# One table for ScalarE's softmax steps in a fused dynamic-convolution and maxout kernel

## The chip, the core and the metric

The kernel runs on one core of a Trainium2 chip. The core has five engines with a queue each: TensorE (PE, matrix products; PEld is its loading of weights), VectorE (DVE), ScalarE (ACT), GpSimd (POOL) and SyncE (SP). They run side by side and wait for one another through semaphores. An engine takes its instructions in the order in which the program issued them. [...]

The metric is the time of one execution on the device in microseconds (us), lower is better. The kernel before takes 410.58 us, the median of three runs (410.37 to 411.28).

## The reference

For each of 8 x 4160 positions a softmax over 7 taps is taken for each of 8 heads, and the 192 channels (24 to a head) are filtered with these taps, over the position itself and the six before it. Then a maxout layer follows:

```python
w = np.exp(weight_gen - max); w = w / (sum(w) + 1e-09)      # 8 heads x 7 taps a position
out = np.einsum('bshk,bskhg->bshg', w, x_unf)               # a causal convolution, 192 channels
h1 = x @ w1                                                  # 192 -> 1024
h2 = x @ w2
g = np.maximum(h1, h2)
return (g @ w_out).astype(np.float32)                        # 1024 -> 192
```

There are 33,280 positions in all. Types outside are float32; the kernel works in bfloat16 where it multiplies.

## The kernel before

The 33,280 positions stand on 128 partitions, 260 columns each. The columns are cut into 17 batches: 16 of 16 columns, and a last one of 4 (`BATCHES`). From the third batch on a batch goes through the engines in two halves (units) of 8 columns; a half begins at column 0 or 8 of its batch.

**The softmax steps of a batch c.** ScalarE takes the exponential of the raw weights (`exp_sum`, L135; named X.c here), VectorE adds up the seven taps of each head (`red`, L147, in two parts), ScalarE takes the logarithm of the sums (`ln`, L151; l.c), VectorE subtracts it from the raw weights (`shift`, L156, in three parts), and ScalarE takes the exponential again (`weights`, L167; W.c.0 for the first half, W.c.8 for the second). So X.c goes to both parts of red, these to l.c, that to shift, and shift to W.c.0 and W.c.8.

**The convolution of a half.** VectorE multiplies inputs by weights (`mul`, L182) and adds the taps in three steps (`adds`, L198, L202, L205). The parts of red for a batch further on stand between these steps of a second half, and the parts of shift between those of a first half. The last addition gives y_t. SyncE's queue issues a DMA that transposes it to yt (`transpose`, L214), with channels on the partitions.

**The maxout on TensorE.** The sum is split as max(h1, h2) = h1 + relu(h2 - h1). The linear part has its own matrix w10 (L347). A tile is one of 8 equal pieces of a half's hidden layer: `hid_tile` (L295) multiplies by the difference of the two weight matrices into one of three PSUM tiles, hda, hdb and hdc, and ScalarE's relu (L305) moves it to SBUF as rd_t. Output columns are added up in PSUM as op_ps (L347, then L335 in two parts, `out_first` and `out_second`), and ScalarE copies them to o_t (`evac`, L391). There is one tile op_ps from group 8 on, so TensorE's first product of a group's output waits for the copy of the group before.

**Groups.** TensorE's work runs in groups (`GROUPS`): 8 of two tiles, then 82 of three or fewer, so that batch 2 begins in group 13. Each group makes its tiles and adds up the output of earlier ones, two or four columns (`OUTS`), from group 23 on by turns. In `hidden` the order on TensorE is hda, hdb, first part of the output, hdc, second part. ScalarE's order is relu of hda, relu of hdb, an empty instruction (`relay`) that tells TensorE that the first part is through, relu of hdc, and the copy.

**Where the softmax steps go.** Up to batch 2, and for l.3, X.3, they are written out by hand. From W.3 on, the code before gives each step a due tile: a formula with the batch number, `AT` with six exceptions, and in `softmax_steps` a rule that puts a long step (X or W) off by a group when the group has four columns and the last one had a long step, but for the groups that start at the tiles in `NOW`. The function `steps` runs them through `beside`, ahead of VectorE's work in `extra`. In a group of four columns `beside` stands before the relu of hdc; in a group of two, behind the copy:

```python
        if len(now) > 2:
            beside()
        relu(rd, t0 + n - 1, 1)
...
            evac(now[0] // 2, len(now) // 2)
        between()
        if len(now) <= 2:
            beside()
```

Of the kernel before, what the change touches and what calls it, by code (L numbers as in the profile page):

```python
# [17 lines left out]
def _sub(base: bass.AP, off: int, dims):  # L18
    ap = [list(base.ap[0])] + [[int(s), int(c)] for s, c in dims]
    return dataclasses.replace(base, offset=base.offset + off, ap=ap)  # L20
# [3 lines left out]
def kernel(  # L24
# [26 lines left out]
    NB = len(BATCHES)  # L51


    def pieces(b):
        n = BATCHES[b][1]
        at, done = [], 0
        for w in (4, 4, 4, 4) if b < 2 else (8, 8) if n == 16 else (n,):
            at.append((done, w))
            done += w
        return at  # L60
# [10 lines left out]
    GROUPS = [(t, 2) for t in range(0, 16, 2)]  # L71
# [59 lines left out]
    def exp_sum(b, i=0, of=1):  # L131
        if i == 0:
            e_ts[b] = pe_.tile([P, BATCHES[b][1] * WGC], FP32, name="e_t", tag="e")
        w = BATCHES[b][1] * WGC // of
        nc.scalar.activation(out=e_ts[b][:, i * w:(i + 1) * w], in_=wg_ts[b][:, i * w:(i + 1) * w], func=AF.Exp)  # L135

    def part(b, i, of):

        n = BATCHES[b][1]
        h0, h1 = n * i // of * H, n * (i + 1) // of * H  # L140
        return slice(h0, h1), h0 * K, [[K, h1 - h0], [1, K]]
# [7 lines left out]
    def ln(b, i=0, of=1):  # L149
        s_t = s_ts[b][:, part(b, i, of)[0]]  # L150
        nc.scalar.activation(out=s_t, in_=s_t, func=AF.Ln)  # L151
# [7 lines left out]
    def weights(b, o):  # L159

        w = dict(pieces(b))[o]
        if b not in en_ts:
            en_ts[b] = pen.tile([P, 16 * WGC * 2], BF16, name="en_t", tag="en")
        J = 2 if w == 4 and b < 2 else 1
        N = w * H // J
        for j in range(J):
            nc.scalar.activation(  # L167
                out=_sub(en_ts[b], (o * WGC + j * N * K) * 2, [[2 * N, K], [2, N], [1, 2]]),
                in_=_sub(wg_ts[b], (o * H + j * N) * K, [[1, K], [K, N], [0, 2]]), func=AF.Exp,
            )  # L170
# [60 lines left out]
    def half(j):  # L231
        return slice(64 * j, 64 * j + 64)
# [33 lines left out]
    def chunks(t):  # L266

        u, k = TILES[t]
        return ([k], 512) if UNITS[u][2] == 8 else ([2 * k, 2 * k + 1], 256)

    def hid_out(t, f, j):

        fs, w = chunks(t)
        hd, at = hd_at[t]
        at += j * 512 + fs.index(f) * w
        return hd[:, at:at + w]
# [5 lines left out]
    def wd_at(j, s, h, c0, n):  # L282

        at = WD[h, j, s] * HF + c0
        return wd[half(j), at:at + n]

    def hid_tile(t):


        u = TILES[t][0]  # L290
        fs, w = chunks(t)
        for f in fs:
            for s in range(3):
                for j in range(2):
                    nc.tensor.matmul(  # L295
                        hid_out(t, f, j), lhsT=wd_at(j, s, f // 4, f % 4 * P, P),
                        rhs=_sub(yt_ts[u][half(j), :], (s + j) % 3 * P, [[3 * P, w // P], [1, P]]),
                        start=(f == fs[0] and s == 0), stop=(f == fs[-1] and s == 2),
                        skip_group_check=True,
                    )  # L300
# [40 lines left out]
    def out_first(now):  # L341

        for c in now[::2]:
            u, i, _ = column(c)
            for s in range(3):
                for j in range(2):
                    nc.tensor.matmul(  # L347
                        op_out(c + j),
                        lhsT=yt_ts[u][half(j), (3 * i + (s + j) % 3) * P:(3 * i + (s + j) % 3 + 1) * P],
                        rhs=w10[half(j), s * D:(s + 1) * D], start=(c == now[0] and s == 0),  # L350
                        stop=False, skip_group_check=True,
                    )
            for f in range(FCH):
                last = [out_hidden(c + j, f, j) for j in range(2)]
        return last
# [10 lines left out]
    def relay(last):  # L366

        go = nc.scalar.nop()
        for mm in last:
            tc.add_manual_dep(go.ins, mm.ins.name, SYNC, reason="bank of the other half")  # L370
        return go
# [52 lines left out]
    OUTS, c = [[], [], []], 0  # L424
    for g in range(3, len(GROUPS)):
        most = 4 if g == 3 else 2 if GROUPS[g][1] == 2 or len(OUTS[-1]) == 4 else 4
        n = min(most, ready[g] - c)
# [5 lines left out]
    def room(g):  # L433

        t0, n = GROUPS[g]
        if "c" in ps:
            for t, k in zip(range(t0, t0 + n), "abc"[:n - 1] + "c"):
                hd_at[t] = ps[k].tile([P, 1024], FP32, name="hd" + k, tag=k), 0
        else:
            for t in range(t0, t0 + n):  # L440
                hd_at[t] = ps["h"].tile([P, 1024], FP32, name="hdp", tag="hd"), 0
        rd = prd.tile([P, 3 * 1024], BF16, name="rd_t", tag="rd")
        for t in range(t0, t0 + n):
            rd_at[t] = (rd, t - t0)
        return rd

    def out_room(now, tag=None):
        tag = tag or ("r" if "r" in ps else "o")
        tile_ = ps[tag].tile([P, 1024], FP32, name="op_ps", tag=tag if tag in "abc" else "op")
        for c in now:  # L450
            op_at[c // 2] = tile_, (c - now[0]) // 2 * D

    def hidden(g, now=(), between=lambda: None, beside=lambda: None, ahead=lambda: None):


        t0, n = GROUPS[g]
        rd = room(g)
        for t in range(t0, t0 + n - 1):
            hid_tile(t)
        if now:  # L460
            out_room(now, "a" if n == 1 and "a" in ps else None)
            last = out_first(now)
        for t in range(t0, t0 + n - 1):
            relu(rd, t, 1)
        if now:
            go = relay(last)
        hid_tile(t0 + n - 1)
        if len(now) > 2:
            beside()
        relu(rd, t0 + n - 1, 1)  # L470
        ahead()
        if now:
            out_second(now, go)
            evac(now[0] // 2, len(now) // 2)
        between()
        if len(now) <= 2:
            beside()

# [214 lines left out]
    def end_of_1():  # L693
# [13 lines left out]
        7: (lambda: (sum_transpose(7)), none),  # L707
    }

    NOW = (28, 40, 49)  # L710
    AT = {
        ('W', 8, 8): 115,
        ('W', 11, 8): 163,
        ('W', 14, 8): 211,
        ('X', 6, 0): 49,
        ('X', 5, 0): 37,
        ('W', 3, 8): 30,
    }
    due = {}
    for c in range(3, NB):  # L720
        soon = c < 8
        parts_ = [(AT.get(('W', c, 0), 16 * (c - 2) + (8 if soon else 10 if c < NB - 1 else 15)), True, lambda c=c: weights(c, 0))]
        if 8 in dict(pieces(c)):
            parts_.append((AT.get(('W', c, 8), 16 * (c - 2) + (14 if soon else 15)), True, lambda c=c: weights(c, 8)))
        if c > 3:
            ln_at = -2 if c == 4 else 0 if c < 8 else 2 if c < 11 else 4
            parts_.append((AT.get(('l', c, 0), 16 * (c - 2) + ln_at), False, lambda c=c: ln(c)))
            parts_.append((AT.get(('X', c, 0), 16 * (c - 3) + (4 if c < 8 else 7)), True, lambda c=c: exp_sum(c)))
        for t, *step in parts_:
            due.setdefault(t, []).append(step)  # L730
    waiting, long_in_two = [], [False]

    def softmax_steps(g):

        t0, n = GROUPS[g]
        for t in range(max(t0, 16), t0 + n):
            waiting.extend(due.get(t, ()))
        two = len(OUTS[g]) <= 2
        put_off = [w for w in waiting if w[0] and not two and long_in_two[0] and t0 not in NOW]
        now = [w for w in waiting if w not in put_off]  # L740
        waiting[:] = put_off
        for _, step in now:
            step()
        long_in_two[0] = two and any(long for long, _ in now)

    def extra(t):

# [17 lines left out]

    def steps(g, tiles):

        if tiles:
            softmax_steps(g)
        for t in tiles:  # L770
            extra(t)

# [5 lines left out]
    for g in range(4, len(GROUPS)):  # L778
        if GROUPS[g][1] == 3 and "c" not in ps:
            later_ps()  # L780
        tiles = [t for t in range(GROUPS[g][0], sum(GROUPS[g])) if t >= 16]
        if g == 9:
            behind(relu_of[16], load_x(3, 0, 8))
        if g in early:
            hidden(g, OUTS[g], early[g][0], ahead=lambda: {4: lambda: (weights(1, 12), ln(2)), }.get(g, none)())
            early[g][1]()
            steps(g, tiles)
        else:
            hidden(g, OUTS[g], beside=lambda: steps(g, tiles))
    rest_of_results(OUTS[-1])  # L790

# [28 lines left out]
```

## Time and profile before

| | before |
|---|---|
| median of three runs | 410.58 us (410.37 to 411.28) |
| the profiled execution | 409.7 us |
| its span on the core | 407.9 us |
| VectorE busy | 370.6 us (91%) |
| ScalarE busy | 361.4 us (89%) |
| GpSimd busy | 74.9 us (18%) |
| TensorE's granted clock | 1.00 |

The span runs from the program's first instruction to its last; 1.8 us of the execution lie around it. The profile's page lists each engine's busy time, the chain of work that ended last, the groups of instructions and their idle time. The trace behind it has every instruction: a row of the timeline gives its start and its length in us, the engine, the line of the kernel, the operation, the tile that is written, the tile that is read, and how often; in brackets behind it, how long the engine had been idle and what ended that. TensorE's matmuls overlap, so a block of them is best read by the time from its start to the next block's start.

### The profile page before, as it was taken

What the parts mean: (1) busy time and instruction counts of PE and PEld (TensorE: products, weight loads), DVE (VectorE), ACT (ScalarE), POOL (GpSimd) and SP (SyncE); (2) the same over time, 40 slices, a digit from 0 to 9 for tenths busy, and PEclk for the clock granted to TensorE, in tenths of its full rate; (3) what the DMA queues carried; (4) which work ended last, traced back from release to release, by engine and by line L of the source; (5) the groups of instructions that cost most, each with busy time, mean ns of one, the idle gap of its engine ahead of it and who ended that gap; (6) DMA issues with size and microseconds to landing.
All of it is one profiled execution on the core that took longest, in us unless ns stands there. A gap on an engine that the chain in (4) does not pass through costs nothing.

```text
span 407.9 us, 16236 instructions
## 1 busy us (share of the span) xinstructions
PE 398.3 (98%) x7458; PEld 317.9 (78%) x7458; DVE 370.6 (91%) x215; ACT 361.4 (89%) x462; POOL 74.9 (18%) x101
## 2 busy tenths in 40 slices
PE   7999999999999999999999999999999999999996
PEld 2689999777777877777787778877787777777795
DVE  5999997999999999999999999999999999999100
ACT  5899889999999999989999999999999889887872
POOL 0311012222211022212102222221122212010000
PEclk9999999999999999999999999999999999999999
DMA  8957497667647854964785497478649647853614
GB/s 240 233 127 212 120 151 162 161 149 183 150 98 213 211 133 101 257 152 104 206 229 123 93 262 172 81 235 215 106 98 258 167 53 248 149 98 85 209 38 159
DMA packets 60785, 65.70 MB, mean 161 GB/s; under 512 B 47631, under 2 KB 49039, under 8 KB 60718
## 3 DMA queue, kind: packets, MB, share of 16 engines
q1 hardware_dynamic: 52334, 40.54, 35.4%
q0 software_dynamic: 8240, 24.04, 29.6%
q8 instruction: 58, 0.95, 0.9%
q10 hardware_dynamic: 144, 0.10, 0.1%
q14 instruction: 9, 0.07, 0.1%
HBM read 35.96 MB, written 25.56 MB: 151 GB/s over the span
## 4 chain that ended last, share of the span: by engine, by line
DVE 66%; PE 23%; issue 5%; ACT 4%; DMA 1%; DVEq 0%; SPq 0%
DVE m_t L182 32%; DVE m_t L198 15%; DVE m_t L202 10%; PE op_ps L335 9%; DVE y_t L205 3%; DVE sum_t L147 3%; PE warm L605 3%; DVE wg_t L156 3%; PE hdc L295 2%; PE hda L295 2%; ACT rd_t L305 2%; PE hdb L295 2%; PE op_ps L347 2%; PE yps L244 2%; PE hdp L295 1%
## 5 line engine op out<-in xcount | busy, mean ns | idle before, releaser
L335 PE MATMUL op_ps<-wo,rd_t 64*128 64x192 bf16 x4160 | 210.7, 243 | 0.5 <-issue 0.4
L335 PEld LDWEIGHTS <-rd_t 64*128 64x128 bf16 x4160 | 180.5, 94 | 16.7 <-issue 0.6
L182 DVE TENSOR_TENSOR m_t<-xb_t,en_t 128x10752 bf16<-128x10752 bf16 (+1 forms) x37 | 187.5, 5071 | 3.1 <-ACT en_t L167 2.8
L295 PEld LDWEIGHTS <-wd 64*128 64x128 bf16 x1776 | 92.9, 94 | 41.9 <-issue 2.1
L305 ACT ACTIVATE rd_t<-hdc 128x1024 bf16<-128x1024 f32 x82 | 84.0, 1025 | 20.4 <-PE hdc L295 18.5
L222 POOL CAST gate<-yt 128x1 f32<-128x1 bf16 x29 | 40.3, 1389 | 263.7 <-DMA yt<-y_t 263.7
L305 ACT ACTIVATE rd_t<-hda 128x1024 bf16<-128x1024 f32 x81 | 83.4, 1030 | 0.4 <-PE hda L295 0.4
L305 ACT ACTIVATE rd_t<-hdb 128x1024 bf16<-128x1024 f32 x81 | 83.6, 1032 | 0.0
L198 DVE TENSOR_TENSOR m_t<-m_t 128x4608 bf16<-128x4608 bf16 (+1 forms) x29 | 72.7, 2508 | 0.1
L295 PE MATMUL hdc<-yt,wd 64*128 64x512 bf16 (+1 forms) x534 | 67.9, 359 | 0.7 <-DMA yt<-y_t 0.7
L391 ACT COPY o_t<-op_ps 128x384 f32<-128x384 f32 (+1 forms) x99 | 55.9, 576 | 13.9 <-PE op_ps L335 13.9
L295 PE MATMUL hda<-yt,wd 64*128 64x512 bf16 (+1 forms) x528 | 67.1, 359 | 0.2 <-DMA yt<-y_t 0.2
L295 PE MATMUL hdb<-yt,wd 64*128 64x512 bf16 (+1 forms) x522 | 67.1, 361 | 0.0
L347 PE MATMUL op_ps<-w,yt 64*128 64x192 bf16 x780 | 55.4, 243 | 0.4 <-ACT w L658 0.4
L347 PEld LDWEIGHTS <-yt 64*128 64x128 bf16 x780 | 38.7, 94 | 16.1 <-issue 0.8
L202 DVE TENSOR_TENSOR m_t<-m_t 128x3072 bf16<-128x3072 bf16 (+1 forms) x29 | 49.9, 1722 | 0.1
L167 ACT ACTIVATE en_t<-wg_t 128x896 bf16<-128x896 f32 (+2 forms) x45 | 35.1, 806 | 0.6 <-PE op_ps L335 0.6
L205 DVE TENSOR_TENSOR y_t<-m_t 128x1536 bf16<-128x1536 bf16 (+1 forms) x29 | 27.3, 940 | 0.5
L114 POOL DMA_DIRECT2D xb_t<-in_x_dram x33 | 17.7, 535 | 31.5 <-ACT rd_t L305 20.4
L156 DVE TENSOR_TENSOR wg_t<-wg_t,sum_t 128x280 f32<-128x280 f32 (+5 forms) x46 | 22.0, 481 | 0.3 <-ACT sum_t L151 0.3
L147 DVE TENSOR_REDUCE sum_t<-e_t 128x64 f32<-128x448 f32 (+2 forms) x31 | 19.6, 633 | 2.9 <-ACT e_t L135 2.8
L135 ACT ACTIVATE e_t<-wg_t 128x896 f32<-128x896 f32 (+2 forms) x18 | 15.9, 887 | 2.7 <-DMA wg_t<-in_weight_gen_dram 2.7
(49 smaller groups left out, 118.3 us busy)
## 6 DMA issues: line engine op xcount, KB each, us to landing
out_dram<-o_t SPq DMA_DIRECT2D x27, 768.0 KB, 5.2
xb_t<-in_x_dram POOLq DMA_DIRECT2D x30, 384.0 KB, 4.9
wg_t<-in_weight_gen_dram POOLq DMA_DIRECT2D x14, 448.0 KB, 5.3
xb_t<-xb_t POOLq DMA_DIRECT2D x16, 288.0 KB, 5.1
out_dram<-o_t SPq DMA_DIRECT2D x10, 384.0 KB, 2.9
wg_t<-in_weight_gen_dram SPq DMA_DIRECT2D x2, 448.0 KB, 4.6
xs<-in_x_dram SPq DMA_DIRECT2D x2, 384.0 KB, 5.9
xb_t<-in_x_dram POOLq DMA_DIRECT2D x3, 192.0 KB, 4.2
```

The source lines that it names most:

```text
L156: nc.vector.tensor_tensor(out=w_t, in0=w_t, in1=_sub(s_ts[b], hs.start, [[1, hs.stop - hs.start], [0, K]]), op=ALU.subtract)
L167: nc.scalar.activation(out=_sub(en_ts[b], (o * WGC + j * N * K) * 2, [[2 * N, K], [2, N], [1, 2]]), in_=_sub(wg_ts[b], (o * H + j * N) * K ...
L182: return nc.vector.tensor_tensor(out=m_out, in0=x_in, in1=_sub(en_ts[b], o * WGC * 2, [[2, K * n * H], [0, G // 2], [1, 2]]), op=ALU.mult,)
L198: nc.vector.tensor_tensor(out=taps(0, 1, 3), in0=taps(0, 1, 3), in1=taps(3, 1, 3), op=ALU.add)
L202: nc.vector.tensor_tensor(out=taps(0, 2, 2), in0=taps(0, 2, 2), in1=taps(1, 5, 2), op=ALU.add)
L205: nc.vector.tensor_tensor(out=_sub(y_ts[b], o * D, [[64, 2], [P, 3 * w // 2], [1, 64]]), in0=taps(0, 1, 1), in1=taps(2, 1, 1), op=ALU.add,)
L222: nc.gpsimd.tensor_copy(out=gate, in_=yt[:, 0:1])
L295: nc.tensor.matmul(hid_out(t, f, j), lhsT=wd_at(j, s, f // 4, f % 4 * P, P), rhs=_sub(yt_ts[u][half(j), :], (s + j) % 3 * P, [[3 * P, w // ...
L305: relu_of[t0] = nc.scalar.activation(out=rd[:, k * 1024:(k + n) * 1024], in_=hd[:, at:at + n * 1024], func=AF.Relu)
L335: return nc.tensor.matmul(op_out(c), lhsT=rd[half(r), k * 1024 + at:k * 1024 + at + P], rhs=wo[half(r), f * D:(f + 1) * D], start=False, s ...
L347: nc.tensor.matmul(op_out(c + j), lhsT=yt_ts[u][half(j), (3 * i + (s + j) % 3) * P:(3 * i + (s + j) % 3 + 1) * P], rhs=w10[half(j), s * D: ...
L391: nc.scalar.copy(out=_sub(o, c % 24 * D, [[D, len(qs)], [h * D, 2], [1, D]]), in_=_sub(tile_, at + (qs[0] - p) * D, [[D, len(qs)], [512, 2 ...
```

## The change

All softmax steps from W.3 on come from one table, `SOFTMAX_AT`, by group and place. Place 0 is before the relu of a group's last tile, place 1 behind the copy, and now each of them can be had in any group. VectorE's `extra` stays where it was.

```diff
@@ hidden
+               before=lambda: None, after=lambda: None):
...
         hid_tile(t0 + n - 1)
+        before()
         if len(now) > 2:
             beside()
         relu(rd, t0 + n - 1, 1)
...
         between()
+        after()
         if len(now) <= 2:
             beside()
@@
-    def softmax_steps(g):
...
-        put_off = [w for w in waiting if w[0] and not two and long_in_two[0] and t0 not in NOW]
...
+    SOFTMAX_AT = {
+        (9, 1): "X.4 W.3.0", (12, 0): "W.3.8 l.4", (15, 1): "X.5", (16, 0): "W.4.0", (16, 1): "l.5",
+        (18, 1): "W.4.8", (19, 0): "X.6", (21, 1): "W.5.0", (23, 1): "W.5.8 l.6", (25, 1): "X.7",
+        (27, 1): "W.6.0", (29, 0): "l.7", (29, 1): "W.6.8 X.8", (33, 1): "W.7.0", (34, 0): "l.8",
+        (35, 1): "W.7.8", (37, 1): "X.9 W.8.0", (39, 1): "W.8.8", (40, 0): "l.9", (41, 1): "X.10",
+        (43, 1): "W.9.0", (44, 1): "l.10", (45, 1): "W.9.8", (47, 1): "X.11", (49, 1): "W.10.0",
+        (51, 0): "l.11", (51, 1): "W.10.8 X.12", (53, 1): "W.11.0", (55, 1): "W.11.8", (56, 0): "l.12",
+        (57, 1): "X.13", (59, 1): "W.12.0", (61, 1): "W.12.8", (62, 0): "l.13", (63, 1): "X.14",
+        (65, 1): "W.13.0", (67, 1): "W.13.8 l.14", (69, 1): "X.15 W.14.0", (72, 0): "l.15",
+        (73, 1): "W.14.8 X.16", (76, 0): "W.15.0", (78, 0): "l.16", (79, 1): "W.15.8", (82, 0): "W.16.0",
+    }
+
+    def softmax_steps(g, place):
+        for step in SOFTMAX_AT.get((g, place), "").split():
+            kind, c, *o = step.split(".")
+            {"W": weights, "l": ln, "X": exp_sum}[kind](int(c), *map(int, o))
@@ steps
-        if tiles:
-            softmax_steps(g)
@@ the loop over groups
-            hidden(g, OUTS[g], beside=lambda: steps(g, tiles))
+            hidden(g, OUTS[g], beside=lambda: steps(g, tiles), before=lambda: softmax_steps(g, 0),
+                   after=lambda: softmax_steps(g, 1))
```

The same instructions are issued on every engine, 434 rows on ScalarE among them. The order on TensorE, VectorE, GpSimd and SyncE is the same as before; on ScalarE these steps stand elsewhere (group, place):

| step | before | after | step | before | after |
|---|---|---|---|---|---|
| W.3.0 | 11, 1 | 9, 1 | l.11 | 52, 0 | 51, 0 |
| l.5 | 18, 1 | 16, 1 | X.12 | 53, 1 | 51, 1 |
| l.6 | 24, 0 | 23, 1 | l.12 | 57, 1 | 56, 0 |
| l.7 | 29, 1 | 29, 0 | X.13 | 59, 1 | 57, 1 |
| X.8 | 31, 1 | 29, 1 | W.14.0 | 71, 1 | 69, 1 |
| l.8 | 35, 1 | 34, 0 | l.14 | 68, 0 | 67, 1 |
| W.8.0 | 39, 1 | 37, 1 | l.15 | 73, 1 | 72, 0 |
| W.8.8 | 41, 1 | 39, 1 | X.16 | 75, 1 | 73, 1 |
| X.10 | 43, 1 | 41, 1 | W.15.0 | 75, 1 | 76, 0 |
| l.10 | 46, 0 | 44, 1 | W.15.8 | 77, 1 | 79, 1 |
| W.11.0, W.11.8 | 55, 1 and 57, 1 | 53, 1 and 55, 1 | | | |

W.3.0 makes the weights of columns 48 to 55. W.15.0 and W.15.8 are the steps that move later, by half a group and by two.

More of the change, by code (lines that the diff above doesn't have):

```diff
@@ L451, in out_room, with hidden @@
             op_at[c // 2] = tile_, (c - now[0]) // 2 * D
-    def hidden(g, now=(), between=lambda: None, beside=lambda: None, ahead=lambda: None):
+    def hidden(g, now=(), between=lambda: None, beside=lambda: None, ahead=lambda: None,
+               before=lambda: None, after=lambda: None):
         t0, n = GROUPS[g]
@@ L708 @@
     }
[L710 to L717, printed above, removed]
-    }
[L719 to L731, printed above, removed]
-    def softmax_steps(g):
[L735 to L738, printed above, removed]
-        put_off = [w for w in waiting if w[0] and not two and long_in_two[0] and t0 not in NOW]
[L740 to L744, printed above, removed]
+    SOFTMAX_AT = {
[9 rows of a table added]
+    }
+    def softmax_steps(g, place):
+        for step in SOFTMAX_AT.get((g, place), "").split():
+            kind, c, *o = step.split(".")
+            {"W": weights, "l": ln, "X": exp_sum}[kind](int(c), *map(int, o))
     def extra(t):
```

## The prediction

> **What bounds the kernel now.** I read the page's totals first, then the chain of waits, the list of waits, and the timeline where these pointed.
>
> ```profile
> span 407.9 us, 16236 instructions
> ...
> PE 398.3 (98%) x7458; PEld 317.9 (78%) x7458; DVE 370.6 (91%) x215; ACT 361.4 (89%) x462; POOL 74.9 (18%) x101
> ...
> DVE 66%; PE 23%; issue 5%; ACT 4%; DMA 1%; DVEq 0%; SPq 0%
> ```
>
> The totals name TensorE, the chain that ended last names VectorE. Both are right, in turn. In the middle of the kernel both are full:
>
> ```profile
> 74.40:328.90 254.50, 254.50 (x4430) 199.30 (x4427) 254.12 (x142) 236.33 (x290) 52.68 (x63) 1.00 0.67 165
> ```
>
> The columns are the stretch, its length, then the busy time of PE, PEld, DVE, ACT and POOL, and the granted clock (1.00). Since matmuls overlap, a full PE may still be a waiting one, so I checked its pace, by the first block (hda) of some groups:
>
> ```profile
> 74.40 0.83 PE L295 MATMUL hda<-yt,wd 64*128 64x512 bf16 x6
> ...
> 303.13 0.83 PE L295 MATMUL hda<-yt,wd 64*128 64x512 bf16 x6
> ...
> 308.21 0.83 PE L295 MATMUL hda<-yt,wd 64*128 64x512 bf16 x6
> ...
> 311.72 0.83 PE L295 MATMUL hda<-yt,wd 64*128 64x512 bf16 x6
> ...
> 328.89 0.83 PE L295 MATMUL hda<-yt,wd 64*128 64x512 bf16 x6
> ```
>
> These are groups 14, 68, 69, 70 and 74. A group of four columns takes 308.21 - 303.13 = 5.08 us, one of two 311.72 - 308.21 = 3.51. From group 14 to 74 there are 28 of four and 32 of two: 28 x 5.08 + 32 x 3.51 = 254.6, and the trace has 328.89 - 74.40 = 254.49. So for sixty groups TensorE never waits, and whatever ScalarE or VectorE lose or gain in there is free. What can be gained are the waits outside this stretch. The list of waits from 70 to 400 us has two of TensorE that matter, and one of VectorE from just before, at 67 us:
>
> ```profile
> DVE m_t L182 <- ACT en_t L167: 2.8, 1, 2.8
> ...
> PE hdc L295 <- DMA yt<-y_t: 0.7, 1, 0.7
> ...
> PE hda L295 <- DMA yt<-y_t: 0.2, 1, 0.2
> ```
>
> TensorE waits late in the kernel for transposed halves, thus for VectorE. VectorE works without a break from 67 us on, so its own wait for the weights W.3.0 is carried to that place. That is the chain's 66%.
>
> **The change, part by part.**
>
> *W.3.0 two groups sooner.* VectorE had ended its last addition and stood idle until W.3.0 came:
>
> ```profile
> 63.76 0.96 DVE L205 TENSOR_TENSOR y_t<-m_t 128x1536 bf16<-128x1536 bf16 x1
> 67.56 5.76 DVE L182 TENSOR_TENSOR m_t<-xb_t,en_t 128x10752 bf16<-128x10752 bf16 x1 [2.85 <-ACT en_t L167]
> ```
>
> In ScalarE's queue it now stands behind X.4 instead of here at 66.50:
>
> ```profile
> 57.24 0.96 ACT L135 ACTIVATE e_t<-wg_t 128x896 f32<-128x896 f32 x1
> ...
> 66.50 1.03 ACT L167 ACTIVATE en_t<-wg_t 128x896 bf16<-128x896 f32 x1
> ```
>
> X.4 ends at 58.20, W.3.0 then by 59.2, and the multiplication starts at 64.7: VectorE gains 2.8 us there.
>
> *How much of the lead lasts.* Half a batch on, VectorE needs X.5, which the table leaves in its place:
>
> ```profile
> 79.38 5.75 DVE L182 TENSOR_TENSOR m_t<-xb_t,en_t 128x10752 bf16<-128x10752 bf16 x1
> 85.05 0.61 DVE L147 TENSOR_REDUCE sum_t<-e_t 128x64 f32<-128x448 f32 x1
> ...
> 82.25 0.96 ACT L135 ACTIVATE e_t<-wg_t 128x896 f32<-128x896 f32 x1
> ```
>
> With 2.8 us of lead the sum would start at 82.25, but X.5 ends at 83.21. So VectorE waits about 1 us, and the lead shrinks to 85.05 - 83.21 = 1.84 us. X.5 is the only step left in place that comes within 2 us of its reader; those that were close later on (l.8, l.11, l.12, X.10, W.8.0) are the ones the table takes forward, so I carry 1.8 us to the end.
>
> *What the lead is worth.* The first late half is the second of batch 13, wanted by the last tile of group 74:
>
> ```profile
> 327.01 0.96 DVE L205 TENSOR_TENSOR y_t<-m_t 128x1536 bf16<-128x1536 bf16 x1
> ...
> 331.35 0.84 PE L335 MATMUL op_ps<-wo,rd_t 64*128 64x192 bf16 x16
> 332.86 0.82 PE L295 MATMUL hdc<-yt,wd 64*128 64x512 bf16 x6 [0.68 <-DMA yt<-y_t]
> ```
>
> y_t ends at 327.97, the transposed half is there 4.9 us later. Sixteen matmuls of L335 take 0.66 us of pace, so hdc would have started at 332.01: 0.85 us lost. The next is wanted by group 80:
>
> ```profile
> 349.98 0.96 DVE L205 TENSOR_TENSOR y_t<-m_t 128x1536 bf16<-128x1536 bf16 x1
> ...
> 354.85 0.84 PE L335 MATMUL op_ps<-wo,rd_t 64*128 64x192 bf16 x16
> 355.93 0.61 PE L295 MATMUL hda<-yt,wd 64*128 64x512 bf16 x4 [0.24 <-DMA yt<-y_t]
> ```
>
> By the same count 355.93 - (354.85 + 0.66) = 0.42 us. With a lead of 1.8 the first half lands about 1.0 us ahead of need. The second lands at 354.1, and TensorE, 0.85 us earlier by then, wants it at 354.7. Both waits go: 1.27 us. VectorE's remaining lead is worth nothing more, since TensorE is then full to the end. What is late next is none of VectorE's halves but TensorE itself.
>
> *Group 12, relieved.* Here a group of four columns with W.3.8, l.4 and a copy in two pieces comes right behind W.3.0, and ScalarE is late:
>
> ```profile
> 69.22 1.05 ACT L167 ACTIVATE en_t<-wg_t 128x896 bf16<-128x896 f32 x1
> 70.13 0.34 ACT L151 ACTIVATE sum_t<-sum_t 128x128 f32<-128x128 f32 x1
> ...
> 71.23 0.90 ACT L391 COPY o_t<-op_ps 128x384 f32<-128x384 f32 x2
> ...
> 71.36 0.89 PE L295 MATMUL hdb<-yt,wd 64*128 64x512 bf16 x6
> 72.19 0.34 PE L347 MATMUL op_ps<-w,yt 64*128 64x192 bf16 x4
> ```
>
> L347 needs op_ps, free at 72.13; at pace (0.65 behind hdb) it would start at 72.01. That is 0.18 us. Without W.3.0 ahead, W.3.8 still stands behind the empty instruction that waits for TensorE, so ScalarE gains only some 0.15 us here. I take 0.15; the bounds are 0 and 0.18.
>
> *Two long steps in one place.* The table puts X and W together behind the copies of groups 9, 29, 37, 51, 69 and (with the short X.16) 73. Each time a group of four columns follows, and two steps of 1.0 us stand before its relus. Before, this occurs too, at group 43:
>
> ```profile
> 200.92 0.96 ACT L135 ACTIVATE e_t<-wg_t 128x896 f32<-128x896 f32 x1
> 201.77 1.03 ACT L167 ACTIVATE en_t<-wg_t 128x896 bf16<-128x896 f32 x1
> ...
> 205.40 0.84 ACT L391 COPY o_t<-op_ps 128x768 f32<-128x768 f32 x1
> ...
> 206.46 0.34 PE L347 MATMUL op_ps<-w,yt 64*128 64x192 bf16 x4
> ```
>
> The copy ends at 206.24, 0.22 us before op_ps is wanted, and group 44 lies inside the sixty groups without a wait. So I cost the pairs at nothing; the cover is those 0.22 us. A pair that starts late by d costs d - 0.22, and with no cover at all one W (1.03 us less 0.1 of overlap) would cost 0.9.
>
> *W.14.0, the step with the least room.* In group 69 it would start at 313.4, right behind X.15, but needs the last part of shift for batch 14:
>
> ```profile
> 312.55 0.96 ACT L135 ACTIVATE e_t<-wg_t 128x896 f32<-128x896 f32 x1
> ...
> 314.75 0.50 DVE L156 TENSOR_TENSOR wg_t<-wg_t,sum_t 128x336 f32<-128x336 f32 x1
> ```
>
> That ends at 315.25, with the lead at 313.4: just in time. Behind a waiting W.14.0 stand the relus of group 70 and the copy that TensorE's group 71 needs. Without lead it would wait 1.85 us and cost 1.85 - 0.22 = 1.6. So the early steps live on the lead that the first one makes.
>
> *Later steps.* W.15.0 and W.15.8 move back; W.15.0 has the room:
>
> ```profile
> 339.46 1.03 ACT L167 ACTIVATE en_t<-wg_t 128x896 bf16<-128x896 f32 x1
> ...
> 350.85 5.75 DVE L182 TENSOR_TENSOR m_t<-xb_t,en_t 128x10752 bf16<-128x10752 bf16 x1
> ```
>
> It ends at 340.50 and is read 10.4 us later; half a group (some 2 us) and the lead (1.8) leave 6. W.15.8 stood two groups (5.08 + 3.51 = 8.6 us) behind W.15.0 and goes two more back, to end near 357.7; it is read one half after 350.85, and two halves are 349.98 - 327.01, so one is 11.5 us: at 362.3, with the lead at 360.5. That leaves 2.8 us. Both cost nothing. The logarithms are a third of a microsecond each, and stand where ScalarE waits for hdc or in a group without a long step: nothing. No DMA is issued by a moved step; the transposes move with VectorE.
>
> *The sum.* 0.85 + 0.42 + 0.15 = 1.42 us. The profiled span 407.9 becomes 406.5, its execution 409.7 becomes 408.3. The median of the runs shown is 0.9 us above that execution, so I forecast 410.58 - 1.42 = 409.2 us. Bounds: 0 to 2.8 us of lead give 0 to 1.27 us; the pairs and W.14.0 take 0 to 1.6 each.
>
> [...]
>
> **The rivals.**
>
> *VectorE sets the end (408.6).* If TensorE's blocks hide waits, the lead of 1.8 us comes off the end whole, and the 0.15 of group 12 beside it: 410.58 - 1.95 = 408.6. The chain's 66% of VectorE speaks for it, the pace against it. Chance 0.10.
>
> *The lead is spent on the way (410.2).* Another step than X.5 proves late for VectorE, ahead of group 74, until the lead is 0.3 us or less: only about 0.4 us is won. For it speaks that one step, X.5, already takes 1 us; against it, that most of those close to their reader were moved forward. This is also how it would be if the early W.3.0 did not start VectorE early, because something else than W.3.0 held it at 64.7. The list has no other wait there. Chance 0.20.
>
> *The pairs hold up TensorE (slower, 411.9).* One mechanism: in the groups behind a pair, ScalarE's copy of op_ps comes later than in group 44, because the second step of the pair waits for VectorE's shift or the queue starts late. Place: groups 30, 38, 52, 70. It decides from 0.22 us of lateness on. At half the bound, 0.9 - 0.22 = 0.68 us each, four cost 2.7 against a gain of 1.42: 410.58 + 1.3 = 411.9. For it speaks W.14.0, which has no room; against it, groups 44, 60 and 76 before, behind pairs, which lie within or beside stretches at full pace. [...] Chance 0.08.
>
> **How the numbers follow.** My forecast has 0.62, the three rivals 0.10, 0.20 and 0.08. What a measurement of this kernel can tell from no change is about 0.2%, 0.8 us, so "faster" begins under 409.8. The forecast with its own spread (408.8 to 409.8) and the first rival are faster: 0.62 + 0.10 less 0.02 for a lead that half lasts, 0.70. The second rival and that 0.02 are the same: 0.22. Slower: 0.08. The range reaches from 408.4, just under the first rival, to 410.6, which takes in the second and leaves the slower one out.
>
> **What would show it.** In the changed profile VectorE's wait for W.3.0 at 67 us is gone, and one of about 1 us for X.5 stands near 82. The two waits of TensorE for transposed halves are gone from the list, group 74's hdc follows its L335 at pace, and the last of TensorE's groups start 1.4 us sooner. The copy behind each pair ends before TensorE's L347 starts at pace. I am wrong if TensorE shows waits for ScalarE in groups 30, 38, 52 or 70, if VectorE's lead at the second half of batch 13 (y_t ends at 327.97 before) is under 1.3 us, or if the time falls by more than 1.7 us, in which case VectorE set the end.

## The result, and the profile after

| | before | after |
|---|---|---|
| median of 22 runs each | 410.51 us (409.47 to 411.96) | 409.45 us (408.25 to 410.96) |
| after / before | | 0.9975, 95% interval 0.9964 to 0.9985 |
| the profiled execution | 409.7 us | 409.29 us |
| its span | 407.9 us | 407.5 us |

The changed kernel is faster by 1.06 us (0.6 to 1.5 by the interval). The forecast was 409.2 us from 410.58, a ratio of 0.9966, which lies inside the interval.

The profiled span fell by 0.4 us alone, and the first thing to see is why. Both kernels are the same up to group 9. Here is the timeline of TensorE at the first hda block of group 8 and of group 87, after:

```profile
50.33 0.84 PE L295 MATMUL hda<-yt,wd 64*128 64x256 bf16 x12
...
386.34 0.86 PE L295 MATMUL hda<-yt,wd 64*128 64x512 bf16 x6
```

and the same two blocks before:

```profile
49.34 0.84 PE L295 MATMUL hda<-yt,wd 64*128 64x256 bf16 x12
...
386.78 0.81 PE L295 MATMUL hda<-yt,wd 64*128 64x512 bf16 x6
```

Group 8 began 0.99 us later in the profiled execution of after, in a part that nobody touched. From group 8 to group 87 TensorE took 386.78 - 49.34 = 337.44 us before and 386.34 - 50.33 = 336.01 after: 1.43 us less. By the starts of the groups' first blocks, 0.15 us of this lies in group 13 (3.69 us before, 3.54 after), 0.85 in group 74 (5.93 and 5.08) and 0.42 in group 79, up to the start of group 80 (3.93 and 3.51), as the sum had it; every other group takes the same time in both, to 0.01 us. I use the distance below, since it leaves the start out. Clock times of after in the rows below are to be read as about 1 us late against before.

The page's totals and the chain of waits, after:

```profile
span 407.5 us, 16242 instructions
...
PE 397.9 (98%) x7458; PEld 342.6 (84%) x7458; DVE 370.9 (91%) x215; ACT 361.6 (89%) x462; POOL 74.0 (18%) x101
...
PE 91%; ACT 4%; DMA 2%; SPq 1%; issue 1%; DVE 0%; DVEq 0%
```

Busy times of PE, DVE and ACT hardly moved, but the chain that ended last went from 66% VectorE to 91% TensorE. VectorE's row is still 91% busy: it no longer sets the end because it is early, not because it works less.

The list of waits from 50 to 400 us, after (engine, line, what was waited for; us in total, times, longest):

```profile
DVE sum_t L147 <- ACT e_t L135: 0.9, 1, 0.9
PEld L335 <- issue: 0.6, 1, 0.6
...
DVE wg_t L156 <- ACT sum_t L151: 0.2, 1, 0.2
```

The 2.8 us of VectorE for W.3.0 and the two of TensorE for transposed halves (0.7 and 0.2) are gone. The timeline shows where W.3.0 now stands, and what VectorE waits for in its place:

```profile
58.24 0.96 ACT L135 ACTIVATE e_t<-wg_t 128x896 f32<-128x896 f32 x1
59.09 1.02 ACT L167 ACTIVATE en_t<-wg_t 128x896 bf16<-128x896 f32 x1
...
64.55 0.96 DVE L205 TENSOR_TENSOR y_t<-m_t 128x1536 bf16<-128x1536 bf16 x1
65.42 5.75 DVE L182 TENSOR_TENSOR m_t<-xb_t,en_t 128x10752 bf16<-128x10752 bf16 x1
...
83.14 0.96 ACT L135 ACTIVATE e_t<-wg_t 128x896 f32<-128x896 f32 x1
...
84.13 0.62 DVE L147 TENSOR_REDUCE sum_t<-e_t 128x64 f32<-128x448 f32 x1 [0.88 <-ACT e_t L135]
```

W.3.0 ends at 60.11, the multiplication follows the last addition at once, and at X.5 VectorE waits 0.88 us. And the places of the two late halves, groups 74 and 80:

```profile
326.12 0.96 DVE L205 TENSOR_TENSOR y_t<-m_t 128x1536 bf16<-128x1536 bf16 x1
...
332.18 0.88 PE L335 MATMUL op_ps<-wo,rd_t 64*128 64x192 bf16 x16
...
332.84 0.86 PE L295 MATMUL hdc<-yt,wd 64*128 64x512 bf16 x6
...
349.08 0.96 DVE L205 TENSOR_TENSOR y_t<-m_t 128x1536 bf16<-128x1536 bf16 x1
...
354.84 0.87 PE L335 MATMUL op_ps<-wo,rd_t 64*128 64x192 bf16 x16
...
355.50 0.86 PE L295 MATMUL hda<-yt,wd 64*128 64x512 bf16 x6
```

Both times the block of L295 follows its sixteen matmuls of L335 by 0.66 us, at pace and with no wait.

### The profile page after: what moved, and what is told of

It is laid out like the page before. It is cut to its first block, busy times and chain, and to the rows that moved or that the text cites. A ratio compares the mean times of both kernels' runs of the same rounds, so it can differ in the third digit from the quotient of the medians.

```text
span 407.5 us, 16242 instructions
## 1 busy us (share of the span) xinstructions
PE 397.9 (98%) x7458; PEld 342.6 (84%) x7458; DVE 370.9 (91%) x215; ACT 361.6 (89%) x462; POOL 74.0 (18%) x101
## 4 chain that ended last, share of the span: by engine, by line
PE 91%; ACT 4%; DMA 2%; SPq 1%; issue 1%; DVE 0%; DVEq 0%
PE op_ps L335 42%; PE hdc L295 13%; PE hda L295 13%; PE hdb L295 13%; PE op_ps L347 8%; ACT rd_t L305 2%; DMA ws1T<-in_moe_w_dram 2%; PE yps L244 1%; PE hdp L295 1%; SPq L542 1%; ACT yt L251 1%; ACT w1t L668 0%; ACT e_t L135 0%; ACT en_t L167 0%; SPq L534 0%
## 5 line engine op out<-in xcount | busy, mean ns | idle before, releaser
L335 PE MATMUL op_ps<-wo,rd_t 64*128 64x192 bf16 x4160 | 217.9, 243 | 0.5 <-issue 0.4
L335 PEld LDWEIGHTS <-rd_t 64*128 64x128 bf16 x4160 | 190.5, 94 | 11.2 <-issue 0.6
L295 PEld LDWEIGHTS <-wd 64*128 64x128 bf16 x1776 | 112.4, 94 | 26.7 <-issue 0.9
L222 POOL CAST gate<-yt 128x1 f32<-128x1 bf16 x29 | 39.2, 1353 | 262.5 <-DMA yt<-y_t 262.5
L295 PE MATMUL hdc<-yt,wd 64*128 64x512 bf16 (+1 forms) x534 | 70.7, 359 | 0.0
L295 PE MATMUL hda<-yt,wd 64*128 64x512 bf16 (+1 forms) x528 | 69.8, 359 | 0.0
L295 PE MATMUL hdb<-yt,wd 64*128 64x512 bf16 (+1 forms) x522 | 69.8, 361 | 0.0
L391 ACT COPY o_t<-op_ps 128x384 f32<-128x384 f32 (+1 forms) x99 | 55.9, 575 | 13.0 <-PE op_ps L335 12.9
L347 PE MATMUL op_ps<-w,yt 64*128 64x192 bf16 x780 | 59.8, 243 | 0.4 <-ACT w L661 0.4
L347 PEld LDWEIGHTS <-yt 64*128 64x128 bf16 x780 | 45.9, 94 | 10.3 <-issue 0.5
```

Of the source, the lines that this page charges most:

```text
L222: nc.gpsimd.tensor_copy(out=gate, in_=yt[:, 0:1])
L295: nc.tensor.matmul(hid_out(t, f, j), lhsT=wd_at(j, s, f // 4, f % 4 * P, P), rhs=_sub(yt_ts[u][half(j), :], (s + j) % 3 * P, [[3 * P, w // ...
L335: return nc.tensor.matmul(op_out(c), lhsT=rd[half(r), k * 1024 + at:k * 1024 + at + P], rhs=wo[half(r), f * D:(f + 1) * D], start=False, s ...
L347: nc.tensor.matmul(op_out(c + j), lhsT=yt_ts[u][half(j), (3 * i + (s + j) % 3) * P:(3 * i + (s + j) % 3 + 1) * P], rhs=w10[half(j), s * D: ...
L391: nc.scalar.copy(out=_sub(o, c % 24 * D, [[D, len(qs)], [h * D, 2], [1, D]]), in_=_sub(tile_, at + (qs[0] - p) * D, [[D, len(qs)], [512, 2 ...
```

## The experiments

Eight kernels ran beside the kernel before; the first four shared 35 runs of it (median 410.30 us), the last four 26 (410.42). "Distance" is that of TensorE from group 8 to group 87, as above. In group 10 TensorE stands for 0.3 to 1.1 us on no semaphore, differently in each execution. The gap is given as what the group took, from its first block to that of group 11, beyond some 5.09 us (groups of four columns take 5.08 to 5.10 without a wait); the last column takes it out.

| kernel | median us (runs) | ratio to before (95%) | group 8 at | distance | gap in group 10 | distance less gap |
|---|---|---|---|---|---|---|
| before | 410.51 (22) | | 49.34 | 337.44 | 0.58 | 336.86 |
| after | 409.45 (22) | 0.9975 (0.9964 to 0.9985) | 50.33 | 336.01 | 0.58 | 335.43 |
| e0_again | 409.19 (12) | 0.9975 (0.9948 to 1.0001) | 49.53 | 336.07 | 0.59 | 335.48 |
| e1_w30_alone | 410.41 (12) | 1.0007 (0.9989 to 1.0025) | 50.56 | 337.06 | 0.86 | 336.20 |
| e2_w30_back | 410.31 (12) | 1.0008 (0.9994 to 1.0021) | 50.40 | 337.37 | 0.31 | 337.06 |
| e3_x5_early | 409.46 (12) | 0.9986 (0.9967 to 1.0004) | 49.90 | 335.92 | 0.31 | 335.61 |
| e4_w14_waits | 411.77 (7) | 1.0040 (1.0009 to 1.0071) | 50.36 | 338.97 | 0.86 | 338.11 |
| e5_three_steps | 409.92 (10) | 0.9994 (0.9976 to 1.0011) | 49.60 | 337.05 | 0.86 | 336.19 |
| e6_16_more | 414.04 (1) | | 54.45 | 336.48 | 1.07 | 335.41 |
| e7_seven_moves | 408.82 (12) | 0.9975 (0.9958 to 0.9992) | 49.79 | 336.04 | 0.58 | 335.46 |

**The changed kernel again (e0_again).** No edit.

> The changed kernel once more, unaltered. Measure beside the time: from the first hda block of group 8 to that of group 87 on TensorE, 337.44 us in the profile before and 336.01 in the profile after, while group 8 began at 49.34 before and at 50.33 after, in a part of the program that the change does not touch. Theory: the 1.43 us between the groups are the change, the 0.99 us ahead of them are chance; so again 336.0 between the groups, a first group between 49.2 and 50.5, and 1.0 to 1.5 us off the time. Rival: the later start belongs to the changed program; then group 8 begins at 50.3 again.

Group 8 began at 49.53 and the distance was 336.07, as in the first profile of after to 0.06 us. So the later start is chance and the shorter distance is not. TensorE waited 0.06 us for the half of group 80, of which more below.

**W.3.0 alone (e1_w30_alone).** The kernel before, with one more exception:

```diff
     AT = {
+        ('W', 3, 0): 21,
```

> The kernel before with one step moved: W.3.0 in group 9 behind X.4, all others by the old due tiles. Theory: VectorE gains 2.8 us, X.5 cuts this to 1.8, l.5 to 1.3, W.8.0 to 1.1, and l.8, which stood 0.09 us ahead of its reader, to 0.1. So TensorE's wait at the end of group 74 is still there with about 0.75 us and that of group 80 with 0.4; between groups 8 and 87 about 337.2 us; the time falls by 0.2 to 0.3 us, no more than can be told from nothing. Rival: W.3.0 is the whole change; 336.0 us between the groups and 1.4 us off the time.

The list of waits from 50 to 400 us, and the longest of VectorE's on the timeline:

```profile
DVE wg_t L156 <- ACT sum_t L151: 2.0, 3, 1.1
...
PE hdc L295 <- DMA yt<-y_t: 0.6, 1, 0.6
```

```profile
168.88 0.31 ACT L151 ACTIVATE sum_t<-sum_t 128x128 f32<-128x128 f32 x1
...
169.22 0.45 DVE L156 TENSOR_TENSOR wg_t<-wg_t,sum_t 128x280 f32<-128x280 f32 x1 [1.13 <-ACT sum_t L151]
```

VectorE had the same 2.8 us of lead, lost 0.9 to X.5 and then 2.0 to three logarithms: 0.44 to l.4, which the change leaves in its place, 0.43 to l.5 and 1.13 to l.8. Group 74 lost 0.72 us again (expected: 0.75), so hardly any lead was left there. The wait at group 80 went, against the expectation: the half was there about 0.5 us sooner behind its addition than in the kernel before (below). Less the gap, the distance is 0.66 us under before, 0.42 of it by that half, and the times show no gain. So the lead of W.3.0 lasts to group 74 only if logarithms behind it move as well.

**Everything but W.3.0 (e2_w30_back).** The changed kernel, with W.3.0 where it stood:

```diff
-        (9, 1): "X.4 W.3.0", (12, 0): "W.3.8 l.4", ...
+        (9, 1): "X.4", (11, 1): "W.3.0", (12, 0): "W.3.8 l.4", ...
```

> The changed kernel with W.3.0 back in group 11; the other moved steps stay early. Theory: without the lead the early steps find VectorE late and hold up ScalarE's queue: l.5 waits about 1.1 us for red behind group 16, W.14.0 some 1 us for shift behind group 69, and each costs TensorE about 0.8 us, while the two waits for transposed halves go since TensorE comes later. Between groups 8 and 87 about 337.8 us, 0.4 more than before; the time 0 to 0.6 us above before. Rival: the other moves are worth something by themselves, or nothing; 336.0 to 337.4 us between the groups and a time of 0 to 1.4 us below before.

The timeline at l.5, in its new place behind W.4.0:

```profile
89.49 0.31 ACT L151 ACTIVATE sum_t<-sum_t 128x128 f32<-128x128 f32 x1 [1.12 <-DVE sum_t L147]
...
92.42 0.49 ACT L391 COPY o_t<-op_ps 128x384 f32<-128x384 f32 x1
...
92.96 0.42 PE L347 MATMUL op_ps<-w,yt 64*128 64x192 bf16 x6 [0.46 <-ACT o_t L391]
```

ScalarE stands 1.12 us at a logarithm whose sums are not there, the copy behind it comes late, and L347 of group 18 with it: TensorE's pace loses 0.85 us there. And W.14.0, which I had priced at 1.6 us without the lead:

```profile
313.50 0.44 DVE L156 TENSOR_TENSOR wg_t<-wg_t,sum_t 128x280 f32<-128x280 f32 x1
...
315.06 1.03 ACT L167 ACTIVATE en_t<-wg_t 128x896 bf16<-128x896 f32 x1
...
315.53 0.50 DVE L156 TENSOR_TENSOR wg_t<-wg_t,sum_t 128x336 f32<-128x336 f32 x1
```

It carries no wait, and it starts 0.97 us before the third part of shift ends (315.53 + 0.50). A batch has 16 columns, the parts of shift are 5, 5 and 6 of them, and W.14.0 reads the first 8: two parts are enough. Group 74 lost 0.61 us:

```profile
327.79 0.96 DVE L205 TENSOR_TENSOR y_t<-m_t 128x1536 bf16<-128x1536 bf16 x1
...
334.28 0.82 PE L295 MATMUL hdc<-yt,wd 64*128 64x512 bf16 x6 [0.45 <-DMA yt<-y_t]
```

Two things meet here. The lead was not there: at pace, and already 0.85 us late, hdc would have started 4.9 us behind the end of y_t (328.75), while in after it stands 5.8 us behind it. And the transposed half came 5.5 us behind y_t, where it took 4.9 in the kernel before; with that time the loss would have been about nothing, as the expectation had it, and with the lead 5.5 would have done as well. 0.85 + 0.61 + 0.15 (group 13, as before) = 1.61 us over after, and the distances less their gaps differ by 337.06 - 335.43 = 1.63. Without W.3.0 the other moves bring nothing that these runs can tell.

**More lead for VectorE (e3_x5_early).** The changed kernel, X.5 two groups sooner:

```diff
-(15, 1): "X.5"
+(13, 1): "X.5"
```

> The changed kernel with X.5 two groups sooner, behind group 13, so that VectorE does not wait for it. Theory: VectorE's lead at the second half of batch 13 grows from 1.9 to about 2.6 us (measured from TensorE's groups), and nothing else changes, as TensorE is full: 336.0 us between groups 8 and 87, the time of the changed kernel within 0.2 us. Rival: VectorE sets the end; the 0.7 to 1.0 us of lead come off the time.

VectorE's wait for X.5 is gone. The half of group 74 in this kernel:

```profile
324.52 0.96 DVE L205 TENSOR_TENSOR y_t<-m_t 128x1536 bf16<-128x1536 bf16 x1
...
331.67 0.84 PE L335 MATMUL op_ps<-wo,rd_t 64*128 64x192 bf16 x16
...
332.33 0.83 PE L295 MATMUL hdc<-yt,wd 64*128 64x512 bf16 x6
```

The addition started 1.60 us sooner than in after, of which 0.43 is the earlier group 8; VectorE is 1.17 us further ahead. The blocks of L335 and L295 stand at 0.66 us as in after: the lead bought nothing. The distance less gap is 0.18 us longer, lost in group 15, because X.5 now stands ahead of a group of two columns, whose copy comes sooner. VectorE does not set the end.

**A step that waits (e4_w14_waits).** The changed kernel, W.14.0 a group too soon:

```diff
-(67, 1): "W.13.8 l.14", (69, 1): "X.15 W.14.0"
+(67, 1): "W.13.8 l.14", (68, 1): "W.14.0", (69, 1): "X.15"
```

> The changed kernel with W.14.0 another group sooner, behind group 68, where it has to wait for VectorE. W.14.0 uses the heads of the first half alone, so of shift's three parts it needs the first two; the second ends near 312.3 us on the clock of the changed kernel's profile, while group 68's copy ends near 310.1. Theory: ScalarE's queue holds everything behind the waiting step: W.14.0 runs from 312.3 to 313.3, the relus of group 69 come 3.2 us late, and its copy ends 2.6 us after TensorE wants op_ps for group 70. So TensorE loses 2.4 to 2.8 us at groups 69 and 70, between groups 8 and 87 it takes 338.6 us and the time rises by 2.6 us over the changed kernel's (1.5 over before). Rival: relus that are ready go ahead of the waiting step, or there is slack of 2 us in ScalarE's queue; 336.0 to 336.6 us.

```profile
312.12 0.45 DVE L156 TENSOR_TENSOR wg_t<-wg_t,sum_t 128x280 f32<-128x280 f32 x1
...
312.66 1.03 ACT L167 ACTIVATE en_t<-wg_t 128x896 bf16<-128x896 f32 x1 [2.25 <-DVE wg_t L156]
...
312.87 0.83 PE L335 MATMUL op_ps<-wo,rd_t 64*128 64x192 bf16 x16 [0.45 <-ACTq L368]
...
314.15 0.50 DVE L156 TENSOR_TENSOR wg_t<-wg_t,sum_t 128x336 f32<-128x336 f32 x1
...
314.65 0.82 PE L295 MATMUL hda<-yt,wd 64*128 64x512 bf16 x6 [0.95 <-ACT rd_t L305]
...
316.85 0.42 PE L347 MATMUL op_ps<-w,yt 64*128 64x192 bf16 x6 [0.46 <-ACT o_t L391]
```

W.14.0 waits 2.25 us, and starts 0.09 us after the second part of shift (312.12 + 0.45), long before the third: its need is settled. Behind it, ScalarE's relay, relu and copy are late, and TensorE waits for each of them in turn: 1.80 us of pace in group 69 and 0.89 in group 70, together 2.69; the distances less their gaps differ by 2.68. Behind the step the queue is some 3.3 us late (the relu of hda in group 69 starts at 313.59, and at 310.01 in after, where the group begins 0.29 us sooner): its wait of 2.25 and about its own length. TensorE loses most of that. Nothing in ScalarE's queue passed the waiting step: the block that makes hda of group 69 was through at 310.21 in this kernel (309.34 + 0.87), and its relu, which stands behind W.14.0, started at 313.59.

**Three long steps in one place (e5_three_steps).** The changed kernel, W.8.8 behind X.9 and W.8.0:

```diff
-(37, 1): "X.9 W.8.0", (39, 1): "W.8.8"
+(37, 1): "X.9 W.8.0 W.8.8"
```

> The changed kernel with three long steps in one place: X.9, W.8.0 and W.8.8 behind group 37's copy (W.8.8 comes from group 39). Theory: the pair leaves 0.22 us between the copy of group 38 and TensorE's next need of op_ps, the third step adds 0.91; TensorE loses 0.69 us at the start of group 39's output, 336.7 us between groups 8 and 87, and the time rises by 0.7 us over the changed kernel's. Rival: the room behind a pair is larger than the copy shows; 336.0 us and the changed kernel's time.

First the pair as it is in after, then the three:

```profile
176.03 0.96 ACT L135 ACTIVATE e_t<-wg_t 128x896 f32<-128x896 f32 x1
176.88 1.03 ACT L167 ACTIVATE en_t<-wg_t 128x896 bf16<-128x896 f32 x1
...
180.52 0.83 ACT L391 COPY o_t<-op_ps 128x768 f32<-128x768 f32 x1
...
181.53 0.46 PE L347 MATMUL op_ps<-w,yt 64*128 64x192 bf16 x6
```

```profile
176.43 1.95 ACT L167 ACTIVATE en_t<-wg_t 128x896 bf16<-128x896 f32 x2
...
180.98 0.82 ACT L391 COPY o_t<-op_ps 128x768 f32<-128x768 f32 x1
...
181.85 0.42 PE L347 MATMUL op_ps<-w,yt 64*128 64x192 bf16 x6 [0.55 <-ACT o_t L391]
```

After the pair the copy ends at 181.35, 0.18 us before L347. A third step takes that and TensorE loses 0.77 us in group 39. So two long steps fit ahead of a group of four columns, with a fifth of a microsecond to spare, and three don't.

**Where the gap in group 10 comes from (e6_16_more).** The changed kernel with 16 more instructions on TensorE (8 weight loads and 8 matmuls) early on; their product goes nowhere:

```diff
-    keep_warm(8)
+    keep_warm(16)
```

> The changed kernel with 8 more warming matmuls near the start, 16 instructions on TensorE with their weight loads. In all profiles so far TensorE stands for 0.3 to 0.9 us in the middle of group 10, with no semaphore to wait for, after 13 of a run of 16 matmuls of L335; the first load behind the gap is number 2753 of TensorE's loads and matmuls, and gaps further ahead lie at 1729, 1985 and 2241, steps of 256. Theory: the gap belongs to the number, not to the instruction (a block of 256 instructions that comes late); so it falls behind 5 of the 16 matmuls now, at the same number 2753. Rival: it belongs to those matmuls' data; it stays behind 13 of 16.

After, then this kernel; both show the 16 matmuls of L335 that the gap splits:

```profile
59.86 0.74 PE L335 MATMUL op_ps<-wo,rd_t 64*128 64x192 bf16 x13
...
61.00 0.34 PE L335 MATMUL op_ps<-wo,rd_t 64*128 64x192 bf16 x3 [0.40 <-issue]
```

```profile
63.98 0.41 PE L335 MATMUL op_ps<-wo,rd_t 64*128 64x192 bf16 x5
...
65.28 0.67 PE L335 MATMUL op_ps<-wo,rd_t 64*128 64x192 bf16 x11 [0.89 <-issue]
```

The gap came 8 matmuls sooner in the program's order of work, and at the same number of TensorE's instructions from the start: in both traces 1375 loads and 1375 matmuls lie ahead of it, so that the load behind it is number 2751. (The expectation's 2753 counts two semaphore instructions at the start as well.) In this pair of executions the gap goes with that number and not with the matmul or its data. This kernel began group 8 some 4 us later; about 2 us of that are the eight matmuls themselves (the eight that after has there, L608, take 1.90), and most of the rest is a wait of 2.5 us for VectorE ahead of them. Its one time tells nothing of the change.

**Seven moves of 22 (e7_seven_moves).** The changed kernel, with W.3.0, l.5, l.8, W.8.0, X.10, l.11 and l.12 in the new places and the fifteen other moved steps (the expectation counts fourteen) where they stood before. The lines of its table in which it differs:

```diff
-(23, 1): "W.5.8 l.6", (29, 0): "l.7", (29, 1): "W.6.8 X.8", (39, 1): "W.8.8", (41, 1): "X.10", (44, 1): "l.10",
+(23, 1): "W.5.8", (24, 0): "l.6", (29, 1): "W.6.8 l.7", (31, 1): "X.8", (41, 1): "W.8.8 X.10", (46, 0): "l.10",
...
-(51, 1): "W.10.8 X.12", (53, 1): "W.11.0", (55, 1): "W.11.8", (57, 1): "X.13", (59, 1): "W.12.0",
+(51, 1): "W.10.8", (53, 1): "X.12", (55, 1): "W.11.0", (57, 1): "W.11.8", (59, 1): "X.13 W.12.0",
...
-(67, 1): "W.13.8 l.14", (69, 1): "X.15 W.14.0", (72, 0): "l.15", (73, 1): "W.14.8 X.16", (76, 0): "W.15.0", (79, 1): "W.15.8",
+(67, 1): "W.13.8", (68, 0): "l.14", (69, 1): "X.15", (71, 1): "W.14.0", (73, 1): "W.14.8 l.15", (75, 1): "X.16 W.15.0", (77, 1): "W.15.8",
```

> The changed kernel with only seven of its moves: W.3.0, and those that stood less than 1.9 us ahead of their reader before (l.5, W.8.0, l.8, X.10, l.11, l.12). The fourteen others stand at their old places. Theory: these seven carry the lead from batch 3 to batch 13, so it is the changed kernel's: 336.0 us between groups 8 and 87, no wait of TensorE for a transposed half over 0.1 us, and the changed kernel's time within 0.2 us. Rival: some of the fourteen matter; a wait of 0.2 us or more at group 74 or 80, 336.3 us or more.

The distance, 336.04, and the ratio, 0.9975, are those of the whole change. The other fifteen moves are worth nothing that these runs can tell.

## Why the prediction was right, and where it was not

The sum was 1.42 us; the trace has 1.43 from group 8 to 87, the medians 1.06 (0.6 to 1.5). Step by step:

*W.3.0 sooner gives VectorE 2.8 us: right.* The multiplication follows the last addition at once (65.42).

*X.5 takes about 1 us of it and 1.84 is left to the end: right.* The wait was 0.88. At the half of group 80 VectorE's addition started at 349.08 against 349.98, and with the 0.99 us that group 8 was later, the lead is 1.89 us. "The only step left in place that comes within 2 us" was one too few: VectorE also waited 0.2 us for l.4, in the second entry of its waits above.

*Both waits for transposed halves go, 1.27 us: right, but neither with the room that I gave it.* The first half I had landed 1.0 us ahead of need; it was there 1.9 us ahead, as GpSimd's cast shows, which starts when the half has come:

```profile
330.99 1.80 POOL L222 CAST gate<-yt 128x1 f32<-128x1 bf16 x1 [9.04 <-DMA yt<-y_t]
```

TensorE wanted it at 332.84. The lead gave this half 1.0 us, as I reckoned; the rest came from its transposition, some 3.9 us behind the addition's end (327.08) where it took 4.9 before. The second I had landed 0.6 us ahead of need. It was there 0.1 us ahead: the cast began at 355.50, just when TensorE wanted it, and the trace has the landing itself at 355.38. The addition had ended at 350.04, so the transposition took some 5.4 us, and 5.0 before. In e1 it took 4.4 for the same half, and in e0 TensorE waited 0.06. The term that I took as fixed, issue to landing, is the one that varies, from 3.7 us to 5.4 for this half over the ten kernels. That the wait went whole is luck as well as lead. Here is GpSimd's timeline, after and in e1 (there the addition ended at 352.25):

```profile
355.50 0.26 POOL L222 CAST gate<-yt 128x1 f32<-128x1 bf16 x1 [10.43 <-DMA yt<-y_t]
```

```profile
356.75 1.20 POOL L222 CAST gate<-yt 128x1 f32<-128x1 bf16 x1 [9.48 <-DMA yt<-y_t]
```

*Group 12 relieved by 0.15: right.* From the first block of group 13 to that of group 14 TensorE took 3.69 us before and 3.54 after.

*Pairs cost nothing, with 0.22 us of cover: right.* The cover measured 0.18 at group 38, and e5 shows its other side.

*W.14.0, "the step with the least room": wrong.* I had it read the last part of shift. It reads the first 8 columns, which the first two parts hold, as e2 and e4 show: after, it starts at its own time, and so it does without the lead. The 1.6 us never stood at stake there.

*"The logarithms are a third of a microsecond each ... nothing": wrong without the lead.* I priced their length and not their need. l.5 is the step that lives on VectorE's lead: in e2 it waited 1.12 us and cost 0.85. And it is the other way round for VectorE: in e1 two logarithms in their old places, l.5 and l.8, took 1.56 us of its lead. With the lead and the new places together neither happens, so the sum came out, by a conclusion ("the early steps live on the lead that the first one makes") that was true of another step than the one I named.

*W.15.0 and W.15.8 have room: right*, at 7.2 and 3.7 us.

*The rivals.* That VectorE sets the end fell with e3: 1.17 us more lead, and nothing gained. The share of weight loading decides nothing here: it was 78% before, 84% after, and 78 to 87% over these kernels, for the same 7458 loads (8 more in e6). "The lead is spent on the way" is what e1 shows to be real: it was the change's own logarithms that kept it from coming true. "The pairs hold up TensorE" did not happen; its mechanism, a wait in ScalarE's queue, is about as dear as I priced it: l.5's 1.12 us in e2 cost 0.85, where the wait less the cover would be 0.90.

What stays open: e1's distance less gap is 0.66 us under before, which its ratio (0.9989 to 1.0025) does not show. 0.42 of it hangs on one transposition, which took 4.4 us in the profiled execution; with the 5.0 of the kernel before, group 80 would have waited again and 0.24 would be left, which lies inside the interval. How long it took in the executions without a profile is not known, and the start and the gaps vary by about as much from one to the next, so I have not shown that this accounts for it.

## What to carry to other kernels

When a full engine's occasional waits trace back to one late step far upstream, price the lead that moving this step makes, then walk it down step by step: each producer left in place that comes within the lead of its reader takes a bite, however short it is itself. Price a step in a queue by what it needs and when that is there, not by its length: a logarithm of 0.3 us that waited 1.12 cost 0.85 (e2). And compare executions over a stretch that begins behind the start, since a span carries its chance with it.

## What the runs showed of the hardware

In these ten profiles TensorE stands still, waiting for no semaphore, at instructions that lie 256 or a multiple apart: counted in loads and matmuls, the load behind such a gap is number 1727, 1983, 2239 or 2751. Loading stood for 0.36 us (e2) to 1.59 (e4) at the first of these. At the last, in group 10, the group lost 0.31, 0.58, 0.59, 0.86 or 1.07 us, by the execution, and e6 shows that the gap goes with the number: there the gaps at 1727, 2239 and 2751 kept their numbers, while other stops of TensorE, at 487, 805 and 1007 in other kernels, stood 16 further on, at 503, 821 and 1023. (One gap more, of 1.66 us in e2 at number 705, lies two off the step.) Behind group 10 the pace of the groups shows no such loss: those of four columns without a wait take 5.08 to 5.10 us. Why TensorE stands at these numbers was not shown. Both pages count 58 DMA packets of the kind `instruction` on one queue (q8, 0.95 MB), and TensorE's 7458 loads and 7458 matmuls make 257 to a packet; that a gap is the wait for such a packet is an inference, since no run changed these transfers.

These gaps also made group 8 late in the profile of after: at 1727, 1983 and 2239 they are 1.28 us, none and 0.82 there, and 0.62, 0.38 and none in the kernel before. That is 1.1 us more, and the group started 0.99 us later. They are not all of the start's spread (group 8 at 49.3 to 50.6 us in nine executions that are alike up to there), which is as large as the change's gain: in e1 TensorE also waits 1.30 us for VectorE at 12.9 us, where it stood 0.42 in the kernel before.

Weight loading took 317.9 us before and 342.6 after, for the same loads and the same matmuls; in e6 it was the most of all:

```profile
PE 399.6 (97%) x7466; PEld 358.3 (87%) x7466; DVE 370.9 (90%) x215; ACT 361.5 (88%) x462; POOL 74.9 (18%) x101
```

Nothing of the time went with it: it was 345.5 us in e0 and 319.8 in e3, whose distances are 336.07 and 335.92. So I would not read that share as a distance from the limit without the pace of the matmuls beside it.
